# A tuned attention kernel with a new start, row weights in 256 KB pieces, and keys laid out for 512-byte transfers

## The chip, the cores and the metric

The kernel runs on one core of one Trainium2 chip. The profile shows five engines of this core, which run side by side (in the kernel before PE is busy for 77% of the span, ACT for 65%, DVE for 59% and POOL for 53%): PE (matrix multiply), DVE (vector), ACT (activation functions), POOL (general vector work) and SP (here it only starts DMA transfers). The metric is device time of one execution in microseconds (us); lower is better. Executions of one kernel scatter here by about 2% (the kernel before: 413.71 to 422.22 us). A run is called slow when it is more than 1.5% above the fastest of the same kernel, and fast otherwise.

All ratios below are computed in one way: the mean time of one kernel's fast runs over the mean time of the other kernel's fast runs of the same rounds on the same chip. This is not quite the ratio of the medians quoted beside them, which are taken over all runs. The bracket behind a ratio is its 95% interval.

## The reference

Two blocks are run twice in a row on x of 2048 tokens by 512 columns. Block A is attention with 32 heads of 16 columns and a window of 256 keys. Block B changes a single row: it picks the row with the largest score, sends it through a gated MLP (512 to 1792 and back) and adds the result.

```python
def _A_ref(x, wqkv, wo):
    B, S, D = x.shape
    H = 32; Dh = D // H; W = 256
    qkv = (x @ wqkv).reshape(B, S, 3, H, Dh)  # then transposed: 3, B, H, S, Dh
    q, k, v = qkv[0], qkv[1], qkv[2]
    scores = jnp.einsum("bhqd,bhkd->bhqk", q, k) * (Dh ** -0.5)
    mask = (idx[:, None] - idx[None, :] >= 0) & (idx[:, None] - idx[None, :] < W)
    p = _softmax(jnp.where(mask, scores, -1e9))
    return einsum("bhqk,bhkd->bhqd", p, v) ... @ wo
# ...
x = A_x
x = x + _A_ref(_layernorm(x), A_wqkv, A_wo)
x = x + _B_ref(_layernorm(x), B_w_r, B_w_gate, B_w_up, B_w_down)
x = x + _A_ref(_layernorm(x), A_wqkv, A_wo)
x = x + _B_ref(_layernorm(x), B_w_r, B_w_gate, B_w_up, B_w_down)
```

(The transposes of the reference are written here as comments or "...".)

## The kernel before

The kernel does not write its instructions in program order. It registers operations with their data dependencies, an assumed duration (`dur`) and a priority (`prio`, in units of token tiles of 128). A list scheduler in the kernel file then fixes, before anything runs, the order of each engine's queue. That is the order in which each engine is handed its work.

Keys pass through four steps. A projection leaves 256 tokens of keys for eight heads in PSUM, the memory that PE's results go to, as fp32. DVE casts them to bf16 into `KTN`, in SBUF, the memory that holds the operands. DMA transfers scatter each head into `KBD`, which is block-diagonal: 4 heads by 32 keys form the 128 columns of one stationary operand (the side of a matmul that PE loads first, as its weights), and the rows of other heads stay zero. PE loads such a block as weights and multiplies it with the queries.

```python
self.KTN = self.sb("KTN", [128, 2, 2, 4, 256], BF16)
self.KBD = self.sb("KBD", [128, self.RK, 4, 8, 128], BF16)      # 4 groups, 8 key blocks, 4 heads x 32 keys
# ... qk(): the two casts out of PSUM, 28 times each
S.add("dve", lambda e: e.tensor_copy(out=self.QT[:, s, tok], in_=q()), ..., dur=612, name="evq", prio=at - URG)
S.add("dve", lambda e: e.tensor_copy(out=self.KTN[:, kb, :, s, :], in_=k()), ..., dur=612, name="evk", prio=at - URG)
# ... kscat(): eight DMAs of 32 KB, one for each head
dst = self.KBD[rows, k2, :, :, 32 * (h % 4):32 * (h % 4) + 32].rearrange("p s b k -> p (s b) k")   # runs of 32 keys = 64 bytes
src = self.KTN[rows, (pr // 2) % 2, pr % 2].rearrange("p s (b k) -> p (s b) k", k=32)
# ... scores(): 256 query columns; edges(): the same weights with 32 columns
r = e.matmul(self.PS[:, G.bank + x, W * u:W * u + n], lhsT=self.KBD[rows, k2, s, 4 * (T % 2) + b, :],
             rhs=self.QT[rows, s, q0:q0 + n], ...)
```

The MLP weights come in loads of 896 KB. The priorities that are constants: `LEAD = 1.0` (how early scores are placed), `URG = 1.0` (how early DVE empties PSUM), `PVL = 0.5` (how early P times V is placed).

Of the kernel before, what the change touches and what calls it, by code (L numbers as in the profile page):

```python
# [56 lines left out]
class _Op:  # L57
    __slots__ = ("idx", "eng", "fn", "deps", "dur", "name", "is_dma", "prio", "signals", "count",
                 "dma_sem", "start", "end", "waits", "dma_extra", "force", "group")

    def __init__(self, idx, eng, fn, deps, dur, name, is_dma, prio):
        self.idx = idx
        self.eng = eng
        self.fn = fn
        self.deps = deps
        self.dur = dur
        self.name = name
        self.is_dma = is_dma
        self.prio = prio
        self.signals = False  # L70
        self.count = 0
        self.dma_sem = None
        self.start = 0.0
        self.end = 0.0
        self.waits = None
        self.dma_extra = 0.0
        self.force = None
        self.group = None

# [13 lines left out]
class Sched:  # L93
# [8 lines left out]
    def __init__(self, dma_latency=2700.0, sem_latency=100.0, n_dma_slots=48):  # L102
# [17 lines left out]
    def add(self, eng, fn, reads=(), writes=(), banks=(), dur=100.0, name="", is_dma=False, prio=None, extra_deps=(), group=None):  # L120
# [26 lines left out]
        op.group = group  # L147
        if group is not None:
            group.ops.append(idx)
# [24 lines left out]
    def schedule(self):  # L174
# [54 lines left out]
        done = 0  # L229
        while done < n:  # L230
# [29 lines left out]
            busy_end = st + op.dur  # L260
            op.end = busy_end + ((self.dma_latency + op.dma_extra) if op.is_dma else 0.0)
# [106 lines left out]
    def run_engine(self, e, handle, sems, dma_sems):  # L368
# [13 lines left out]
        if e == "sp":  # L382
            totals = {}
            for i in self.dma_ops:
                o = ops[i]
                if totals.get(o.dma_sem, 0) < o.count:
                    totals[o.dma_sem] = o.count
            for slot, tot in sorted(totals.items()):
                if self.sp_known.get(("dma", slot), 0) < tot:
                    handle.wait_ge(dma_sems[slot], tot)  # L390


NBATCH = 4
CAPS = {"s": 2, "m": 3, "q": 4}
LEAD = 1.0
URG = 1.0
MIL = 0.0
PVL = 0.5
# [5 lines left out]
W = 256  # L404
# [3 lines left out]
class Builder:  # L408
# [16 lines left out]
    def alloc(self):  # L425
# [5 lines left out]
        self.RM = 2  # L431
# [3 lines left out]
        self.MW = self.sb("MW", [128, self.RM, FF * 2], BF16)  # L435
# [4 lines left out]
        self.KBD = self.sb("KBD", [128, self.RK, 4, 8, 128], BF16)  # L440
        self.VN = self.sb("VN", [128, 2, 4, 8, 17], BF16)
        self.VBD = self.sb("VBD", [128, self.RV, 8, 2, 8, 17], BF16)
# [45 lines left out]
        self.mctr = 0  # L488
        self.chunks = {}
# [13 lines left out]
    def init(self):  # L503
# [3 lines left out]
        S.base = -9.0  # L507
        self.load_x(0, -9.5)
        for i, c in enumerate((0, 512, 1024)):
            for h in range(2):  # L510
                S.dma("act" if h else "sp", lambda e, c=c, h=h: e.dma_start(self.WQKV[:, 2 * h:2 * h + 2, c:c + 512],
                                                                            self.A_wqkv[256 * h:256 * h + 256, c:c + 512].rearrange("(kc p) n -> p kc n", p=128)),
                      writes=["wqkv%d_%d" % (i, h)], nbytes=256 * 1024, name="ld_wqkv", prio=-9.3 + 0.3 * i)
            if i == 0:
                self.load_x(2, -9.2)

        wo = self.A_wo.rearrange("(sp q x p) n -> sp q p x n", sp=2, q=4, x=2)
        for i in range(8):
            q, sp = i // 2, i % 2
            S.dma("act", lambda e, q=q, sp=sp: e.dma_start(self.WO[32 * q:32 * q + 32, 2 * sp:2 * sp + 2, :], wo[sp, q]), writes=["wo%d" % i],  # L520
                  nbytes=64 * 1024, name="ld_wo", prio=-7.0)
        S.dma("act", lambda e: e.dma_start(self.WR16[:], self.B_w_r.partition_broadcast(128)),
              writes=["wr16"], nbytes=128 * 1024, name="ld_wr", prio=-6.9)
        for g in range(4, self.RX, 2):
            self.load_x(g, -6.8 + 0.1 * g)
        S.add(P, lambda e: e.memset(self.JUNK[:, 0:128], 1.0), writes=["junk"], dur=100)
        S.add(P, lambda e: e.memset(self.ONEB[:], 1.0), writes=["oneb"], dur=60)
        S.add(P, lambda e: e.memset(self.MHALF[:], -0.5), writes=["mhalf"], dur=60)
        S.add(P, lambda e: e.affine_select(out=self.IDB[:], in_=self.JUNK[:, 0:128], pattern=[[-1, 128]], compare_op=ALU.is_equal,
                                           fill=0.0, base=0, channel_multiplier=1), reads=["junk"], writes=["idb"], dur=300)  # L530
        S.base = -8.0
        S.add(P, lambda e: e.affine_select(out=self.M8[:], in_=self.JUNK[:, 0:8].rearrange("p (a h) -> p a h", a=2), pattern=[[-64, 2], [-16, 4]],
                                           compare_op=ALU.is_ge, fill=0.0, base=0, channel_multiplier=1), reads=["junk"], writes=["m8"], dur=100)
        S.add(P, lambda e: e.affine_select(out=self.M8[:], in_=self.M8[:], pattern=[[64, 2], [16, 4]],
                                           compare_op=ALU.is_ge, fill=0.0, base=15, channel_multiplier=-1), reads=[], writes=["m8"], dur=100)
        S.add(P, lambda e: e.tensor_tensor(out=self.M4[:], in0=self.M8[:, 0, :], in1=self.M8[:, 1, :], op=ALU.add), reads=["m8"], writes=["m4"], dur=100)
        S.add(P, lambda e: e.affine_select(out=self.IDF[:], in_=self.JUNK[:, 0:128], pattern=[[-1, 128]], compare_op=ALU.is_equal,
                                           fill=0.0, base=0, channel_multiplier=1), reads=["junk"], writes=["idf"], dur=300, prio=0.4)

        T = self.XN[:, 1, 0:256].rearrange("p (w h k) -> p w h k", w=2, h=4)  # L540
        S.add(P, lambda e: e.memset(self.XN[:, 1, 0:256], 1.0), writes=["xn#1"], dur=120)
        for w, pat, base, cm, op in ((slice(0, 2), [[0, 2], [-32, 4], [0, 32]], 0, 1, ALU.is_ge), (slice(0, 2), [[0, 2], [32, 4], [0, 32]], 31, -1, ALU.is_ge),
                                     (0, [[32, 4], [1, 32]], 0, -1, ALU.is_ge), (1, [[-32, 4], [-1, 32]], 0, 1, ALU.is_gt)):
            v = T[:, w]
            S.add(P, lambda e, v=v, pat=pat, base=base, cm=cm, op=op: e.affine_select(out=v, in_=v, pattern=pat, compare_op=op, fill=0.0, base=base, channel_multiplier=cm),
                  reads=[], writes=["xn#1"], dur=250)
        S.add("dve", lambda e: e.tensor_reduce(out=self.MSK[:], in_=T.rearrange("p w h k -> p w k h"), axis=AX.X, op=ALU.max), reads=["xn#1"], writes=["msk"], dur=350)

        for p in range(1, self.RK):
            S.add("act", lambda e, p=p: e.memzero(self.KBD[:, p].rearrange("p a b c -> p (a b c)")),  # L550
                  writes=["kbd%d_%d" % (p, h) for h in range(32)], dur=2200, name="zkbd", prio=-8.0 + p)
        for p in range(self.RV):
            S.add("dve" if p else P, lambda e, p=p: e.memset(self.VBD[:, p].rearrange("p a b c d -> p (a b c d)"), 0.0),
                  writes=["vbd%d_%d" % (p, h) for h in range(4)], dur=1200, name="zvbd", prio=-3.5 + p)
        S.add(P, lambda e: e.memset(self.VN[:].rearrange("p a b c d -> p (a b c d)"), 1.0),
              writes=["vn0", "vn1"], dur=560, name="ovn", prio=-3.8)
        for q in range(4):
            v = self.PT[:, PITCH * 24 * q:PITCH * 24 * (q + 1)].rearrange("p (n c) -> p n c", c=PITCH)[:, :, 0:96]
            S.add(P, lambda e, v=v: e.memset(v, 0.0), writes=["pz%d" % q], dur=1500, name="zpt", prio=-3.0 + 0.1 * q)
        S.add(P, lambda e: e.memset(self.PT[:, PITCH * 96:PITCH * 96 + 96], 0.0), writes=["pz4"], dur=60, prio=-2.0)  # L560
# [5 lines left out]
              reads=["wr16"], writes=["swc"], dur=600, prio=-0.5)  # L566
# [15 lines left out]
    def ln(self, g, at):  # L582
# [6 lines left out]
        S.add("dve", lambda e: e.bn_stats(out=self.ST6[:, k4, :], in_=x), reads=[xk], writes=["st6#%d" % k4], dur=612, name="bnst")  # L589
        S.add("dve", lambda e: e.bn_aggr(out=MV[:, k4, :], in_=self.ST6[:, k4, :]), reads=["st6#%d" % k4], writes=["mv#%d" % k4], dur=160)  # L590
        rk = "rs#%d" % k4
        S.add("pool", lambda e: e.tensor_scalar(out=RS[:, k4, 0:1], in0=MV[:, k4, 1:2], scalar1=1.0, scalar2=EPS, op0=ALU.mult, op1=ALU.add),
              reads=["mv#%d" % k4], writes=[rk], dur=220)
        S.add("pool", lambda e: e.tensor_tensor(out=RS[:, k4, 1:2], in0=RS[:, k4, 0:1], in1=self.MHALF[:], op=ALU.pow),
              reads=["mhalf"], writes=[rk], dur=560)
# [51 lines left out]
    def qk(self, b, s, at):  # L647
        S = self.S
        kb = b % 2
        XNT = self.XNT  # L650
        G = S.group("m" if b else "q")

        def f(e, ph, js):
            r = None
# [494 lines left out]
    def build(self):  # L1149
# [20 lines left out]
        for b in range(NW // NBATCH):  # L1170
# [9 lines left out]
            if b:  # L1180
                ev(w - 2.08, self.kscat, 2 * b)
# [1041 lines left out]
```

## Time and profile before

| | before |
|---|---|
| time, median of 3 runs | 416.69 us (413.71 to 422.22) |
| profiled span, granted PE clock | 413.4 us, 0.901 |
| first exponential of the softmax | 30.5 us |
| first and last P times V matmul | 35.5 and 388.5 us |
| DMA packets | 137,854 |
| PE idle put down to "issue" | 28.0 us |

The page of the profile gives each engine's busy time. Below that it cuts the span into 40 equal slices, here of 10.3 us: a digit is the busy share in tenths, for PEclk the granted PE clock in tenths of full speed. From the page of the kernel before:

```profile
span 413.4 us, 20980 instructions
PE 316.3 (77%) x9521; PEld 224.8 (54%) x9521; DVE 243.4 (59%) x601; ACT 268.0 (65%) x298; POOL 219.9 (53%) x403
...
PE   0488998769789678897668987888988876877771
...
ACT  2329978877877377885119749748798875869100
...
PEclk9999999999789898999559998869999996959858
DMA  8444425426676954728895193764447485684060
```

PE is busy 77% of the time, and no engine fills the span. At the left edge PE is idle for the whole first slice (the first matmul starts at 14.7 us), and ACT, which does the exponentials, is at two to three tenths for three. The clock has a dip (5) in the middle.

The chain of waits goes back from the last instruction to whatever released each step. The same page sums it by engine, then by line:

```profile
PE 50%; ACT 16%; DVE 12%; issue 8%; DMA 8%; POOL 2%; SPq 1%; DVEq 0%; POOLq 0%
ACT PT L747 16%; PE PS L833 13%; PE PS L659 11%; PE PS L769 9%; PE PS L872 8%; DMA OT<-ON 6%; PE PS L701 6%; DMA XR<-in_A_x_dram 2%; PE PS L798 2%; PE PS L1050 2%; DVE PT L780 1%; DVE JUNK L895 1%; DVE XR L877 1%; DVE ST6M L893 1%; DVE ON L851 1%
```

The groups of instructions with shapes kept apart show what it and its neighbours cost. Columns are line, engine, operation, tiles, shape and count, then busy us and mean ns, then the engine's idle time just before them and what ended it:

```profile
L769 PEld LDWEIGHTS PS<-QT,KBD 64*128 64x128 bf16 x1024 | 39.4, 97 | 54.1 <-ACT PT L747 34.3 <-issue 6.1 <-DVE ON L851 3.4
L798 PE MATMUL PS<-QT,KBD 64*128 64x32 bf16 x896 | 16.4, 175 | 4.6 <-ACT PT L747 2.4 <-issue 2.0
L798 PEld LDWEIGHTS PS<-QT,KBD 64*128 64x128 bf16 x896 | 14.4, 94 | 9.3 <-ACT PT L747 5.9 <-issue 2.2 <-DVE VN L710 0.4
L685 DVE CAST KTN<-PS 128x512 bf16<-128x512 f32 x28 | 19.0, 677 | 0.0
```

So a load of a key block as weights takes 94 to 97 ns, and an edge matmul 175 ns. For the scatter of the keys, the view of one tile gives the time of the issue on SP (min, median and max, ns) and the time from issue to landing:

```profile
L722 SPq DMA_DIRECT2D KBD<-KTN x120: 591/632/3262, 31.8 to 358.7; - x120
DMA to landing us min/median/max: 2.3/3.1/8.0
```

The table by stretches of time has busy us and counts for PE, weight loads, DVE, ACT and POOL, then granted clock, DMA share and GB/s. It shows the dip in the middle:

```profile
200.00:220.00 20.00, 13.43 (x367) 10.86 (x366) 7.78 (x23) 4.95 (x6) 8.23 (x16) 0.53 0.80 174
```

### The profile page before, as it was taken

The numbers are of one execution on the slowest core, as the hardware profiler recorded it, in microseconds if no ns is written. First come the engines' busy times: TensorE is split into PE (matmuls) and PEld (weight loads), VectorE is DVE, ScalarE is ACT, GpSimd is POOL, SyncE is SP. The second block draws the span as 40 slices with busy tenths as digits, with TensorE's granted clock in tenths as the row PEclk, the third lists the DMA queues.
The fourth block names the chain that finished last, engine by engine and source line by source line (L and its number), as shares of the span: only waits on it lengthen the run. The fifth ranks groups of instructions, "written<-read, shape, count | busy, mean of one in ns | idle before, by whom it ended". The sixth has DMA issues, their size and how long they took to land.

```text
span 413.4 us, 20980 instructions
## 1 busy us (share of the span) xinstructions
PE 316.3 (77%) x9521; PEld 224.8 (54%) x9521; DVE 243.4 (59%) x601; ACT 268.0 (65%) x298; POOL 219.9 (53%) x403
## 2 busy tenths in 40 slices
PE   0488998769789678897668987888988876877771
PEld 0244676556567356566455655636665655646540
DVE  6684565566658264795437687627756563527661
ACT  2329978877877377885119749748798875869100
POOL 9992445464863448555144419927595533527231
PEclk9999999999789898999559998869999996959858
DMA  8444425426676954728895193764447485684060
GB/s 243 125 95 88 74 37 132 87 45 110 136 86 163 223 97 118 153 55 242 94 241 111 60 185 69 154 142 137 65 95 154 121 192 70 144 226 117 22 199 23
DMA packets 137854, 50.94 MB, mean 123 GB/s; under 512 B 114073, under 2 KB 132122, under 8 KB 137757
## 3 DMA queue, kind: packets, MB, share of 16 engines
q1 hardware_dynamic: 136156, 48.07, 54.1%
q8 instruction: 77, 1.26, 1.3%
q10 hardware_dynamic: 1600, 1.44, 1.2%
q14 instruction: 21, 0.16, 0.1%
HBM read 24.00 MB, written 13.95 MB: 92 GB/s over the span
## 4 chain that ended last, share of the span: by engine, by line
PE 50%; ACT 16%; DVE 12%; issue 8%; DMA 8%; POOL 2%; SPq 1%; DVEq 0%; POOLq 0%
ACT PT L747 16%; PE PS L833 13%; PE PS L659 11%; PE PS L769 9%; PE PS L872 8%; DMA OT<-ON 6%; PE PS L701 6%; DMA XR<-in_A_x_dram 2%; PE PS L798 2%; PE PS L1050 2%; DVE PT L780 1%; DVE JUNK L895 1%; DVE XR L877 1%; DVE ST6M L893 1%; DVE ON L851 1%
## 5 line engine op out<-in xcount | busy, mean ns | idle before, releaser
L747 ACT ACTIVATE PT<-PS 128x1024 bf16<-128x1024 f32 (+5 forms) x284 | 258.7, 999 | 96.0 <-PE PS L769 93.1
L833 PE MATMUL PS<-VBD,PT 64*128 64x34 bf16 x5760 | 103.2, 177 | 22.5 <-issue 14.9
L769 PE MATMUL PS<-QT,KBD 64*128 64x256 bf16 (+4 forms) x1024 | 100.6, 279 | 24.6 <-ACT PT L747 15.1
L833 PEld LDWEIGHTS PS<-VBD,PT 64*128 64x128 bf16 x5760 | 97.7, 94 | 39.2 <-issue 21.0
L807 POOL TENSOR_TENSOR PT<-PT,MSK 128x1024 bf16<-128x1024 bf16 x28 | 59.2, 2114 | 41.3 <-ACT PT L747 41.0
L659 PE MATMUL PS<-XNT,WQKV 64*128 64x512 bf16 x512 | 75.4, 387 | 2.2 <-DVE MV L590 1.7
L769 PEld LDWEIGHTS PS<-QT,KBD 64*128 64x128 bf16 x1024 | 39.4, 97 | 54.1 <-ACT PT L747 34.3
L899 POOL TENSOR_SCALAR RSM<-XR 128x1 f32<-128x1 f32 x32 | 9.9, 308 | 103.0 <-DVE XR L894 99.2
L780 DVE TENSOR_TENSOR PT<-PT,MSK 128x512 bf16<-128x512 bf16 x64 | 30.8, 481 | 45.5 <-ACT PT L747 45.3
L872 PE MATMUL PS<-WO,OT 64*128 64x256 bf16 x512 | 46.7, 304 | 12.2 <-DMA OT<-ON 8.7
L701 PE MATMUL PS<-WQKV,XNT 64*128 64x256 bf16 x512 | 47.4, 297 | 4.1 <-issue 3.3
L877 DVE TENSOR_TENSOR XR<-PS,XR 128x512 f32<-128x512 f32 x32 | 22.0, 689 | 29.5 <-PE PS L872 29.5
L872 PEld LDWEIGHTS PS<-WO,OT 64*128 64x128 bf16 x512 | 25.6, 104 | 22.2 <-DMA OT<-ON 9.6
L849 DVE RECIPROCAL RD<-PS 128x16 f32<-128x16 f32 x64 | 15.9, 249 | 34.0 <-PE PS L833 31.8
L659 PEld LDWEIGHTS PS<-XNT,WQKV 64*128 64x128 bf16 x512 | 25.1, 96 | 16.3 <-issue 4.8
L710 DVE CAST VN<-PS 128x512 bf16<-128x512 f32 x32 | 22.0, 689 | 18.4 <-PE PS L701 18.4
L701 PEld LDWEIGHTS PS<-WQKV,XNT 64*128 64x128 bf16 x512 | 25.0, 102 | 13.7 <-issue 4.6
L683 DVE CAST QT<-PS 128x512 bf16<-128x512 f32 x28 | 19.2, 686 | 16.3 <-PE PS L659 16.3
L851 DVE TENSOR_TENSOR ON<-PS,RD 128x256 bf16<-128x256 f32 x64 | 26.9, 420 | 1.2
L895 DVE SCALAR_TENSOR_TENSOR JUNK<-XR,WR 128x512 bf16<-128x512 f32 x32 | 24.6, 768 | 0.0
L602 POOL TENSOR_SCALAR XN<-XR,RS 128x512 bf16<-128x512 f32 (+1 forms) x28 | 22.6, 811 | 2.1 <-DMA XNT<-XN 1.3
L589 DVE BATCH_NORM_STATS2 ST<-XR 128x6 f32<-128x512 bf16 (+1 forms) x32 | 20.9, 672 | 2.9 <-DMA XR<-in_A_x_dram 2.9
(106 smaller groups left out, 289.9 us busy)
## 6 DMA issues: line engine op xcount, KB each, us to landing
scr<-XR SPq DMA_DIRECT2D x13, 516.0 KB, 4.1
vd<-VN SPq DMA_DIRECT2D x16, 272.0 KB, 3.6
VBD<-vd SPq DMA_DIRECT2D x64, 68.0 KB, 2.9
XR<-scr SPq DMA_DIRECT2D x8, 512.0 KB, 4.4
KBD<-KTN SPq DMA_DIRECT2D x120, 32.0 KB, 3.1
MW<-in_B_w_gate_dram SPq DMA_DIRECT2D x4, 896.0 KB, 5.3
MW<-in_B_w_down_dram SPq DMA_DIRECT2D x4, 896.0 KB, 7.3
XR<-in_A_x_dram SPq DMA_DIRECT2D x8, 256.0 KB, 6.7
```

The source lines that it names most:

```text
L602: S.add("pool", lambda e: e.tensor_scalar(out=XN[:, k2, :], in0=x, scalar1=RS[:, k4, 1:2], scalar2=RS[:, k4, 2:3], op0=ALU.mult, op1=ALU.add),
L659: r = e.matmul(self.PS[:, G.bank + w, :], lhsT=self.WQKV[rows, j, 512 * w + 128 * s:512 * w + 128 * s + 128], rhs=XNT[rows, kb, :, j, :], ...
L701: r = e.matmul(o, lhsT=XNT[rows, kb, jt, j, :], rhs=self.WQKV[rows, j, 1024 + 256 * w:1280 + 256 * w], start=(ph == 0 and j == 0), stop=(p ...
L747: return e.activation(out=out, in_=i, func=ACTF.Exp, scale=0.25)
L769: r = e.matmul(self.PS[:, G.bank + x, W * u:W * u + n], lhsT=self.KBD[rows, k2, s, 4 * (T % 2) + b, :], rhs=self.QT[rows, s, q0:q0 + n], s ...
L780: S.add("dve", lambda e: e.tensor_tensor(out=P, in0=P, in1=m, op=ALU.mult), reads=["msk"], writes=["pt%d_%d" % ((4 * t + b) % 12, 2 * sp + ...
L807: S.add("pool", lambda e: e.tensor_tensor(out=P[:, :, :, 0:32], in0=P[:, :, :, 0:32], in1=m, op=ALU.mult), reads=["msk"], writes=key, dur= ...
L833: r = e.matmul(self.PS[:, G.bank + x, 34 * g:34 * g + 34], lhsT=self.PT[rows, c:c + 128], rhs=self.VBD[rows, v3, b8, :, 2 * s + a, :], sta ...
L851: S.add("dve", lambda e: e.tensor_tensor(out=o, in0=acc()[:, :, :, 0:16], in1=rd.unsqueeze(3).broadcast_to([128, 2, 8, 16]), op=ALU.mult), ...
L872: r = e.matmul(self.PS[:, G.bank + w, 0:256], lhsT=self.OT[rows, k2, j, :], rhs=self.WO[rows, j, 256 * w:256 * w + 256], start=(ph == 0 an ...
L877: S.add("dve", lambda e: e.tensor_tensor(out=self.xf(T).rearrange("p (x c) -> p x c", x=2), in0=self.PS[:, G.bank:G.bank + 2, 0:256], in1= ...
L895: S.add("dve", lambda e: e.scalar_tensor_tensor(out=self.JUNK[:], in0=x, scalar=1.0, in1=self.WR16[:], op0=ALU.mult, op1=ALU.mult, accum_o ...
```

## The change

The intent is to start earlier, to shorten DMA work and to keep the queues fed:

1. Start: the first batch's queries and keys are projected in two halves, each after two row tiles; 16 matmuls on constants keep PE busy during the loads; zeroing is done as 32-bit words; small layer-norm operations go from POOL to DVE.
2. Row (MLP) weights come as 256 KB pieces into 7 buffers and, near the end, into space that has come free.
3. Keys are interleaved, key by key, over the eight blocks of 32, so that the scatter moves 512 bytes at a time in place of 64.
4. Order: new priorities, and the scheduler gets a model of instruction fetch, with constants of its own (13.6 ns an instruction).

The diff is cut to its core; parts that only rename or set assumed durations are left out.

```diff
-        self.KBD = self.sb("KBD", [128, self.RK, 4, 8, 128], BF16)
+        self.KBD = self.sb("KBD", [128, self.RK, 4, 4, 256], BF16)
 # ... qk(): the cast of the keys
-        S.add("dve", lambda e: e.tensor_copy(out=self.KTN[:, kb, :, s, :], in_=k()), ..., dur=612, name="evk", prio=at - URG)
+        S.add("dve", lambda e: e.tensor_copy(out=self.KTN[:, kb, :, s, :].rearrange("p a (k b) -> p a b k", b=8), in_=k()), ..., dur=600, name="evk", prio=at - URG)
 # ... the block as PE loads it
+    def keys(self, rows, k2, s, b):
+        return self.KBD[rows, k2, s].rearrange("p h (k b) -> p (h k) b", b=8)[:, :, b]
 # ... kscat()
-                dst = self.KBD[rows, k2, :, :, 32 * (h % 4):32 * (h % 4) + 32].rearrange("p s b k -> p (s b) k")
-                src = self.KTN[rows, (pr // 2) % 2, pr % 2].rearrange("p s (b k) -> p (s b) k", k=32)
+                dst = self.KBD[rows, k2, :, h % 4, :]
+                src = self.KTN[rows, (pr // 2) % 2, pr % 2]
 # ... the first batch in halves, and PE kept busy
+            def warm(e, G=G):
+                for _ in range(4):
+                    r = e.matmul(self.PS[:, G.bank, :], lhsT=self.JUNK[:, 0:128], rhs=self.JUNK[:], start=True, stop=True)
+    def qk_first(self, half, s, at):
 # ... row weights
-        self.MW = self.sb("MW", [128, self.RM, FF * 2], BF16)
+        self.MW = self.sb("MW", [128, 7, 1024], BF16)
 # ... order of the queues
+FETCH_NS = 13.6
+FETCH_AHEAD = 512
-LEAD = 1.0
-URG = 1.0
-MIL = 0.0
-PVL = 0.5
+LEAD = 2.188
+URG = 1.942
+MIL = -0.471
+PVL = 0.507
```

## The prediction

> **What bounds the kernel now** (median 416.7 us, profiled span 413.4). No single engine: the page's busy table has PE 316 us (77%), ACT 268, DVE 243, POOL 220, and the chain of waits is 50% PE, 16% ACT, 12% DVE, 8% "issue", 8% DMA. Time is lost in four places.
>
> 1. Start. The timeline has no matmul before 14.7 us and the first softmax exponential at 30.5. POOL is 9.4 of the first 10 us busy: 2.02 us memsets stand in front of the tiny layer-norm operations, and Q/K of the first batch waits for all four row tiles (PE begins it at 22.3).
> 2. Row-weight loads. They come as two 896 KB DMAs; an attention-output transpose queued behind them took 8.4 us (at 132) and 8.8 us (at 334), against a median of 4.0. PE sat 4.4 us, then ran on.
> 3. Between 194 and 214 the timeline has PE gaps of 2.1, 3.5 and 3.6 us put down to "issue". The stretch table shows PE 13.4 of 20 us busy at a granted clock of 0.53 in 200–220, with the DMA engines saturated just before (1.23 of an engine share, an overlap artefact). [...] The waits view sums PE issue gaps to 28 us.
> 4. Clock. 0.66–0.69 in 110–120, 270–280, 340–350, 0.60 in 360–370: about 20 us of PE busy time runs longer than it need. [...]
>
> **What the change does**
> - Start: 32-bit memsets (1.87–2.02 → about 1.0 us), eps additions on DVE instead of POOL (308 ns POOL → about 0.15), Q/K after two tiles, weights before other loads, 16 warming matmuls. My estimate, from load landings of 5–9 us and 0.85 us per half group: exponentials flow from about 17 us. Gain 13 us, carried through, since what follows is a full pipeline.
> - Key scatter: 64 B runs become 512 B; 120 DMAs × 512 = 61,000 of the 138,000 packets become 7,700. DMA share falls from 54% of 16 engines to about 40%; issue shrinks from 0.63 to about 0.45 us each.
> - Row weights in 256 KB: transposes wait about 1 us, not 4–5. With fewer packets and instruction-aware PE ordering I expect half of items 2–4 back: 13 us.
> - Tail: most down-weights are already there (before, PE waits 1.9 us for them and ends the second down product at 406.8); the final DMA wait moves behind the flag. 4 us.
> - Added: 64 small DVE operations (about 10 us DVE, off the chain), warm matmuls 4–7 us in idle PE, and key weights read with a 16-byte stride: 1,920 weight loads, in this trace 94–97 ns each. [...] The 256-column scores should hide it, the 32-column edges (16 us) may not: 0–10 us, expected 2.
>
> Sum: −13 −13 −4 +2 = −28, so **388 us**, 80% range 373–403. Faster by over 2%: 0.92; within 2%: 0.06; slower: 0.02.
>
> **Right if**: first exponential by 15–19 us; packets near 84,000; PE issue gaps under 16 us; no 20 us stretch at 0.53; output transposes never over 6 us; edge and score groups within 10% busy.
>
> **Wrong if**: strided weight loads double and show as PE time in the edge groups; the earlier start is eaten by an ACT-limited middle; new piece loads collide elsewhere; clock dips move rather than vanish.

Three passages are cut out of it where marked: what the author took to be the cause of the "issue" gaps and of the halved clock, and why strided weight reads should cost time. What the reads do cost was measured afterwards: 150 to 162 ns a load in place of 94 to 97. That half of items 2 to 4 would come back (the second 13), and the +2, were estimates, with no measurement behind them. The "about 20 us" of item 4 is an estimate too: in its four stretches of 10 us, busy time times the clock that is missing comes to about 10 us, and with 200 to 220 to 16. The figures for the change are forecasts; the kernel after has 0.97 us (DVE) and 1.07 us (POOL) for a memset, 0.14 us for an addition on DVE and 0.60 us for an issue of the scatter (medians).

## The result, and the profile after

| | before | after |
|---|---|---|
| time, median | 418.65 us (413.71 to 422.22, 4 runs) | 459.95 us (459.38 to 465.47, 4 runs) |
| ratio | | 1.1108 [1.0948, 1.1268] |
| profiled span, granted clock | 413.4 us, 0.901 | 457.6 us, 0.851 |
| first exponential | 30.5 us | 20.2 us |
| first and last P times V matmul | 35.5 and 388.5 us | 48.5 and 436.6 us |
| DMA packets | 137,854 | 94,813 |
| PE idle put down to "issue" | 28.0 us | 14.4 us |

The median of before differs from the one given above because one more run was taken beside the new kernel. The changed kernel is 11% slower. All four of its runs are fast; of the four of before, the two above 420 us count as slow, so the ratio rests on 413.71 and 416.69 us. The lines that answer to those of before begin with its page; a slice is now 11.4 us:

```profile
span 457.6 us, 21192 instructions
PE 359.3 (79%) x9601; PEld 267.9 (59%) x9601; DVE 296.7 (65%) x676; ACT 273.0 (60%) x303; POOL 194.2 (42%) x334
...
PE   4967977887888779987897866986789786985782
...
ACT  4488236778887487754176524785386768794300
...
PEclk9787789899999997789559987689978999795677
DMA  8423423324257335814596336364545421559041
```

The left edge has filled up as intended. DVE, though, went from 243.4 to 296.7 us. The chain of waits of the kernel after, by engine and by line:

```profile
PE 53%; DVE 28%; ACT 11%; issue 5%; DMA 2%; SPq 0%; DVEq 0%
DVE KTN L717 14%; PE PS L834 11%; PE PS L898 11%; ACT PT L812 11%; PE PS L703 8%; PE PS L762 7%; PE PS L937 6%; PE PS L863 5%; DVE QT L715 4%; PE PS L1178 2%; DVE XR L942 2%; DMA XR<-in_A_x_dram 2%; PE PS L1132 1%; DVE PT L845 1%; DVE KTN L743 1%
```

DVE's share of the chain went from 12% to 28%, and a line that did not show before, the key cast (now line 717), is its largest single term: 14% of 457.6 is 64 us. Taken in order of time, the chain runs through all 28 of these casts. The groups of the kernel after, for the same instructions as before (scores are line 834 now, edges 863, P times V 898, exponentials 812):

```profile
L834 PEld LDWEIGHTS PS<-QT,KBD 64*128 64x128 bf16 x1024 | 61.9, 150 | 72.0 <-ACT PT L812 25.9 <-DVE KTN L717 14.0 <-issue 6.6
L863 PE MATMUL PS<-QT,KBD 64*128 64x32 bf16 x896 | 32.6, 212 | 5.9 <-issue 3.3 <-ACT PT L812 2.5
L863 PEld LDWEIGHTS PS<-QT,KBD 64*128 64x128 bf16 x896 | 31.2, 162 | 9.8 <-ACT PT L812 5.3 <-issue 3.7
L717 DVE CAST KTN<-PS 128x512 bf16<-128x512 f32 x28 | 68.3, 2439 | 0.0
```

One cast takes 2439 in place of 677 ns, so 28 of them are busy 68.3 in place of 19.0 us. Weight loads of keys went from 94–97 to 150–162 ns, and an edge matmul from 175 to 212 ns. The last columns of the score loads already name the cast: 14.0 us of idle time in front of them end with it. A stretch of the chain in order of time (start, us, what) from the kernel after shows how the cast delays PE:

```profile
69.39 0.60 DVE JUNK L962 x2
69.99 0.10 DVE XR L959
70.09 0.57 DVE QT L715
70.66 2.33 DVE KTN L717
...
73.05 0.44 PE PS L834 x4
```

The casts of queries and keys run one behind the other on DVE and PE's scores start when the key cast ends. The view of line 717 sums who waited for it (us, times):

```profile
  PEld PS L834: 14.0, 9
  PE PS L834: 12.2, 9
  PEld PS L898: 4.4, 3
  PE PS L898: 3.8, 3
```

ACT suffers behind PE: its waits for scores went from 93.1 to 127.7 us in the waits view. The key scatter, in the view of its tile, did become cheaper:

```profile
L787 SPq DMA_DIRECT2D KBD<-KTN x120: 590/597/1929, 28.4 to 405.0; - x120
DMA to landing us min/median/max: 2.0/2.6/4.5
```

The dip of the clock is still there, in a later stretch:

```profile
220.00:240.00 20.00, 18.27 (x432) 13.74 (x426) 8.38 (x31) 9.44 (x13) 9.28 (x16) 0.51 0.92 231
```

### The profile page after: what moved, and what is told of

Its sections match the earlier page's. It is cut to its first block, busy times and chain, and to the rows that moved or that the text cites. A ratio compares the mean times of both kernels' runs of the same rounds, so it can differ in the third digit from the quotient of the medians.

```text
span 457.6 us, 21192 instructions
## 1 busy us (share of the span) xinstructions
PE 359.3 (79%) x9601; PEld 267.9 (59%) x9601; DVE 296.7 (65%) x676; ACT 273.0 (60%) x303; POOL 194.2 (42%) x334
## 2 busy tenths in 40 slices
DMA packets 94813, 50.93 MB, mean 111 GB/s; under 512 B 53112, under 2 KB 89081, under 8 KB 94716
## 4 chain that ended last, share of the span: by engine, by line
PE 53%; DVE 28%; ACT 11%; issue 5%; DMA 2%; SPq 0%; DVEq 0%
DVE KTN L717 14%; PE PS L834 11%; PE PS L898 11%; ACT PT L812 11%; PE PS L703 8%; PE PS L762 7%; PE PS L937 6%; PE PS L863 5%; DVE QT L715 4%; PE PS L1178 2%; DVE XR L942 2%; DMA XR<-in_A_x_dram 2%; PE PS L1132 1%; DVE PT L845 1%; DVE KTN L743 1%
## 5 line engine op out<-in xcount | busy, mean ns | idle before, releaser
L812 ACT ACTIVATE PT<-PS 128x1024 bf16<-128x1024 f32 (+5 forms) x284 | 263.3, 986 | 145.2 <-PE PS L834 127.7
L834 PE MATMUL PS<-QT,KBD 64*128 64x256 bf16 (+4 forms) x1024 | 114.7, 311 | 42.6 <-ACT PT L812 13.4
L834 PEld LDWEIGHTS PS<-QT,KBD 64*128 64x128 bf16 x1024 | 61.9, 150 | 72.0 <-ACT PT L812 25.9
L961 POOL TENSOR_TENSOR XR<-XR,MHALF 128x1 f32<-128x1 f32 x32 | 17.8, 555 | 135.0 <-DVE XR L960 123.1
L703 PE MATMUL PS<-XNT,WQKV 64*128 64x512 bf16 x448 | 67.7, 388 | 5.5 <-DVE KTN L717 2.9
L717 DVE CAST KTN<-PS 128x512 bf16<-128x512 f32 x28 | 68.3, 2439 | 0.0
L937 PE MATMUL PS<-WO,OT 64*128 64x256 bf16 x512 | 48.5, 305 | 5.5 <-DVE KTN L717 2.9
L762 PEld LDWEIGHTS PS<-WQKV,XNT 64*128 64x128 bf16 x512 | 28.8, 111 | 15.7 <-issue 5.4
L863 PE MATMUL PS<-QT,KBD 64*128 64x32 bf16 x896 | 32.6, 212 | 5.9 <-issue 3.3
L863 PEld LDWEIGHTS PS<-QT,KBD 64*128 64x128 bf16 x896 | 31.2, 162 | 9.8 <-ACT PT L812 5.3
L771 DVE CAST VN<-PS 128x512 bf16<-128x512 f32 x32 | 22.2, 700 | 16.6 <-PE PS L762 16.4
L703 PEld LDWEIGHTS PS<-XNT,WQKV 64*128 64x128 bf16 x448 | 21.6, 97 | 18.6 <-DVE KTN L717 3.5
L638 POOL TENSOR_TENSOR RS<-RS,MHALF 128x1 f32<-128x1 f32 x32 | 18.6, 592 | 28.5 <-DVE MV L634 18.5
```

The costliest lines, as they stand in the source:

```text
L703: r = e.matmul(self.PS[:, G.bank + w, :], lhsT=self.WQKV[rows, j, 512 * w + 128 * s:512 * w + 128 * s + 128], rhs=XNT[rows, kb, :, j, :], ...
L762: r = e.matmul(o, lhsT=XNT[rows, kb, jt, j, :], rhs=self.WQKV[rows, j, 1024 + 256 * w:1280 + 256 * w], start=(ph == 0 and j == 0), stop=(p ...
L812: return e.activation(out=out, in_=i, func=ACTF.Exp, scale=0.25)
L863: r = e.matmul(self.PS[:, G.bank + x, c:c + 32], lhsT=self.keys(rows, k2, s, 4 * (T % 2) + bb), rhs=self.QT[rows, s, q0:q0 + 32], start=(b ...
L937: r = e.matmul(self.PS[:, G.bank + w, 0:256], lhsT=self.OT[rows, k2, j, :], rhs=self.WO[rows, j, 256 * w:256 * w + 256], start=(ph == 0 an ...
```

## The experiments

The first theory is that the cast's writes with a 16-byte step cost the time. The rival theories are that the weights read with a 16-byte step cost it, or that the new start or the new order does. Eighteen kernels ran, in five sets; the kernel before was run with each set (medians 418.83, 417.02, 418.56 and 418.16 us in the timed ones), and every kernel gave the reference's result. Line 717 is the key cast in all kernels made from the one after, line 685 in those made from the one before.

### Only the cast's direction changed

```diff
-  tensor_copy(out=self.KTN[:, kb, :, s, :].rearrange("p a (k b) -> p a b k", b=8), in_=k())
+  tensor_copy(out=self.KTN[:, kb, :, s, :].rearrange("p a (k b) -> p a k b", b=8), in_=k().rearrange("p a b k -> p a k b"))
```

The first batch's cast was changed in the same way. Layout, weights, transfers and the order of every queue are those of the kernel after; only now the writes are contiguous and the reads from PSUM take the step.

> The changed kernel, but the cast of the keys walks its elements in the other order: it reads PSUM with a stride and writes SBUF contiguously. Layout, DMA runs of 512 B and weight stride of 16 B stay, the result stays right. Theory A (the strided SBUF write of the key cast, 2439 ns instead of 677, 28 times, is the loss): cast back at 0.7 us, time 380 to 405 us, ratio to before 0.91 to 0.97. Rival B (the strided weight loads slow the PE): cast at 0.7 us but time still over 435. Rival C (new order and pieces are what lose): over 445.

Measured: 410.64 us (407.57 to 415.31), 0.9778 [0.9677, 0.9878] of before. The groups of this kernel:

```profile
L863 PEld LDWEIGHTS PS<-QT,KBD 64*128 64x128 bf16 x896 | 30.8, 163 | 9.9 <-ACT PT L812 5.8 <-issue 3.4
L717 DVE CAST KTN<-PS 128x512 bf16<-128x512 f32 x28 | 19.1, 681 | 0.0
```

The cast is back at 681 ns although the step is now on the PSUM side, and 49.3 us of the median are gone (459.95 less 410.64). The weight loads still cost 163 ns. So the cast carries the loss, and the strided weights do not. The time is a little over the 380 to 405 us that theory A expected, and far under the 435 and 445 of its rivals.

### The new layout alone, on the kernel before, with and without the strided cast

```diff
 # kernel before, with the KBD, keys() and kscat() of the change
+  tensor_copy(out=self.KTN[:, kb, :, s, :].rearrange("p a (k b) -> p a b k", b=8), in_=k())                              # first
+  tensor_copy(out=self.KTN[:, kb, :, s, :].rearrange("p a (k b) -> p a k b", b=8), in_=k().rearrange("p a b k -> p a k b"))  # second
```

> The kernel before with the changed key layout alone (512 B runs, strided cast, strided weights). A and B: 450 to 475 us, ratio 1.08 to 1.14, since 28 casts get 1.76 us longer (49 us on DVE) in a kernel whose other queues are as before. C: within 2% of before.

> As e4, but with the cast writing contiguously. A: 400 to 418 us, ratio 0.96 to 1.0, as the 512 B runs help a little. B: 445 or more, close to e4.

Measured: 469.17 us, 1.1144 [1.1007, 1.1281], with the strided cast, and 421.82 us, 1.0108 [1.0021, 1.0194], with contiguous writes. From the groups of the first of the two:

```profile
L685 DVE CAST KTN<-PS 128x512 bf16<-128x512 f32 x28 | 68.2, 2436 | 0.0
```

Nearly all of the 11% comes with the cast, even with old start, old order and old row loads; 47.4 us of it goes when the writes are contiguous. The second kernel also prices the rest of the layout: packets fall by 53,761 to 84,093 and the main queue's share from 54.1% to 50.0%, and yet the time rises by about 1%, while PE's loads of key weights take 149 to 163 ns each. The layout is no gain at all on the kernel before, where theory A had expected a small one, 400 to 418 us: the cast was right, this part was not.

### All of the change but the layout

```diff
 # kernel after, with KTN, KBD, kscat() and the weights of the kernel before
-        return self.KBD[rows, k2, s].rearrange("p h (k b) -> p (h k) b", b=8)[:, :, b]
+        return self.KBD[rows, k2, s, b, :]
```

> The changed kernel with the old key layout whole: 64 B runs, contiguous casts and weights; all else stays changed. A and B: 380 to 405 us. C: over 430. Against e1 it tells what 512 B runs gain less what strided weights cost: A expects the two within 2%; B expects this one 30 us or more below e1. Weight loads of the scores back to 97 ns from 150, of the edges to 94 from 162.

Measured: 405.42 us (403.66 to 408.67), 0.9727 [0.9637, 0.9816]. The queues are in the order of the kernel after. This is 5.2 us below the kernel with contiguous casts, though the intervals overlap. The rest of the change is thus worth about 2.7% (1.8 to 3.6% by the interval), or 11 us of the predicted 28 or so. This kernel is called "old keys" below, and the question becomes where the rest went.

### Middle ways: four and two blocks interleaved

```diff
 # kernel after, contiguous casts; D = 4, then D = 2
-        self.KBD = self.sb("KBD", [128, self.RK, 4, 4, 256], BF16)
+        self.KBD = self.sb("KBD", [128, self.RK, 4, 8 // D, 4, 32 * D], BF16)
-        return self.KBD[rows, k2, s].rearrange("p h (k b) -> p (h k) b", b=8)[:, :, b]
+        return self.KBD[rows, k2, s, b // D].rearrange("p h (k d) -> p (h k) d", d=D)[:, :, b % D]
```

> The changed kernel with keys interleaved four blocks at a time instead of eight: 256 B runs, weights read with a stride of 8 B, casts written contiguously; result right. If the 16-byte stride (one key per 16 bytes) is what slows the weight loads, score loads fall from 149 ns to about 98 and edge loads from 163 to about 94, PE busy from 350 to about 325, time 395 to 405 us. If any stride does it, they stay near 149 and 163 and the time at 405 to 412.

> As the run with four blocks interleaved, with two: 128 B runs, weights read with a stride of 4 B. If only strides that leave fewer than four keys to 16 bytes are slow: score loads 97 to 100 ns (four blocks 116, eight 149), edges 94 to 97, and 400 to 406 us, the fastest so far or level with it.

Measured: 406.05 us, 0.9705 [0.9618, 0.9792], with four blocks (runs of 256 bytes, weights at a step of 8 bytes), and 411.28 us, 0.9879 [0.9764, 0.9993], with two (128 bytes, 4 bytes). The second has 12 first-batch DVE operations more than old keys. Four blocks is level with old keys, and it is the only kernel of those run in rounds whose whole interval lies below 0.98. Two expectations missed: with four blocks the loads went neither back to 98 and 94 ns nor stayed at 149 and 163 (116 and 114), and two blocks, whose loads did come back (98 and 95), took 411.28 us and not the 400 to 406. From the groups of the four-block kernel:

```profile
L840 PEld LDWEIGHTS PS<-QT,KBD 64*128 64x128 bf16 x1024 | 47.9, 116 | 54.0 <-ACT PT L818 30.9 <-issue 7.2 <-DVE QT L715 2.4
```

The mean weight load of the scores was 98 ns with a step of 2 bytes (old keys), 98 with 4, 116 with 8 and 149 with 16.

### Where the write gets dear

```diff
 # four-block and two-block kernels, the key cast iterated so that it writes with a step of 2 * D bytes
-  out=self.KTN[...].rearrange("p a (c k d) -> p a c k d", k=32, d=D), in_=k().rearrange("p a (c d) k -> p a c k d", d=D)
+  out=self.KTN[...].rearrange("p a (c k d) -> p a c d k", k=32, d=D), in_=k().rearrange("p a (c d) k -> p a c d k", d=D)
```

> The four-block kernel (406.05 us, cast 680 ns with contiguous writes) with its key cast iterated so that each step writes 8 bytes further in SBUF (PSUM read in order). If the write cost goes with how far apart two writes lie (16 bytes cost 2439 ns): about half the excess, 1500 to 1700 ns a cast. If any write that isn't contiguous costs the same: about 2440 ns, and about 455 us. If only 16 bytes and more cost: about 680 ns, and 402 to 412 us.

> The same for two interleaved blocks (411.3 us, cast 680 ns with contiguous writes): each step of the cast writes 4 bytes further. If the cost goes with the distance: 900 to 1200 ns. If any write that isn't contiguous costs the same: about 2440 ns, and about 455 us. If only 16 bytes and more cost: about 680 ns, and 405 to 416 us.

Measured: 414.99 us with a step of 8 bytes and 402.96 us with 4 bytes, single runs. Their groups, in this order, one from each kernel:

```profile
L717 DVE CAST KTN<-PS 128x512 bf16<-128x512 f32 x28 | 36.3, 1298 | 0.0
```

```profile
L717 DVE CAST KTN<-PS 128x512 bf16<-128x512 f32 x28 | 20.2, 722 | 0.0
```

A cast of 512 columns takes 680 ns with contiguous writes, 722 with a step of 4 bytes, 1298 with 8 and 2439 with 16. At 8 bytes all three expectations missed: the excess is neither half of that at 16 bytes nor all of it nor none, but a third (618 of 1759 ns). At 4 bytes the third came nearest. From 4 to 8 bytes the cast takes 1.80 times as long, from 8 to 16 bytes 1.88 times; up to 4 bytes only 1.06 times. These are four points: why the cost rises so is not shown, and what a step beyond 16 bytes costs is open, since no run has one.

### Each remaining part undone in the kernel with old keys

```diff
 # old order
-FETCH_NS = 13.6                      +FETCH_NS = 0.0
-LEAD = 2.188, URG = 1.942, MIL = -0.471, PVL = 0.507      +LEAD = 1.0, URG = 1.0, MIL = 0.0, PVL = 0.5   (and the other priorities and assumed DMA latency of before)
 # old row loads: load_mlp, mlp_gu, mlp_act and mlp_down of before, 896 KB each
 # old start: init() of before, the first batch projected whole, V early
```

> The run with the old key layout (405 us) with the old priorities and without the model of instruction fetch in the order of the queues; start and pieces stay changed. If the new order is worth the gain in the middle that the prediction put on it: 410 to 420 us. If the order gives nothing: 402 to 408, and PE idle put down to issue stays within 5 us of that run's.

> The run with the old key layout with the old 896 KB row weight loads; all else as there. If the pieces are worth what the prediction expected [...]: 412 to 420 us and output transposes over 8 us again. If they give little: 402 to 408.

> The run with the old key layout with the old start (loads, memsets, whole first batch, no warming matmuls); all else as there. If the earlier start goes through to the end: first exponential at 29 to 31 us and 413 to 420 us. If the head start is lost soon after (in that run ACT idles 7.1 and 4.2 us between 44 and 59 us while PE does projections): 403 to 409.

Measured: 415.32 us, 0.999 [0.9917, 1.0064], with the old order; 417.59 us, 1.0036 [0.9957, 1.0115], with the old row loads; 417.36 us, 0.9947 [0.9852, 1.0043], with the old start (two of its four runs were slow, the profiled one among them, so its ratio rests on two runs and its trace is not used). The old order leaves PE's "issue" idle time where it was (19.9 us, 19.1 in old keys), and with the old row loads the slowest output transpose lands in 8.5 us again, as expected. Whichever part is taken out, the whole 2.7% goes. Parts whose gains add up do not behave so.

### Single parts put into the kernel before

```diff
 # kernel before with init(), the halves of the first batch and the layer norm of the change
 # kernel before with the 256 KB pieces of the change
```

> The kernel before with the new start alone. If the start's 11 us go through: 403 to 408 us (0.97 to 0.98), first exponential at 19 to 21 us. If the head start is lost later without the other parts: 413 to 420.

> The kernel before with the 256 KB row weight pieces alone. If they are worth 3% by themselves: 402 to 408 us, no output transpose over 7 us and no stretch of 20 us at a granted clock near 0.53. If they pay only together with the new order: 412 to 420.

Measured: 420.06 us, 1.0052 [0.9941, 1.0164], with the new start; 420.33 us, 1.0031 [0.9896, 1.0166], with the pieces. Neither gives anything by itself, though the new start does bring the first exponential from 30.5 to 20.4 us.

### Two priorities nudged

```diff
 # old keys                                   # kernel before
-LEAD = 2.188, PVL = 0.507                    -LEAD = 1.0, PVL = 0.5
+LEAD = 2.1,   PVL = 0.49                     +LEAD = 1.04, PVL = 0.483
```

> The run with the old key layout (405 us), with nothing changed but two priorities by a few per cent (the lead of the scores 2.188 to 2.1, that of PV 0.507 to 0.49): same work, same start, same pieces, a slightly other order. If start, pieces and order are worth 2 to 3% each by themselves: 402 to 408 us. If the order is fitted to the exact program, so that any edit costs what the undone parts cost: 412 to 418.

> The kernel before with two priorities of its order nudged by 3 to 4% (LEAD 1.0 to 1.04, PVL 0.5 to 0.483). If the order of the kernel before is as closely fitted as that of the changed kernel with old keys: slower by 2 to 4%, 428 to 435 us. If it is an ordinary order: 412 to 424 us.

Measured: old keys nudged 420.24 us, 1.0082 [0.999, 1.0174]; before nudged 424.44 us, 1.0183 [1.0088, 1.0279]. A nudge of 3 to 4% in two constants, with no work added or removed, costs old keys its whole gain, 3.6% against its own ratio and more than the 412 to 418 us that the worse expectation gave, and before 1.8%. The second lies under the 2% that was expected of a closely fitted order, and above an ordinary one's; it is between the two readings.

### PE kept busy for longer, and for less long

```diff
-                for _ in range(4):      # 16 warming matmuls in four groups
+                for _ in range(9):      # 36;  in the other kernel range(1): 4
```

> The kernel with the old key layout (405.4 us) with 36 warm-up matmuls in place of 16, which fill the idle gap of 4.3 us after them; the order of every queue is unchanged. If the low clock of the start costs time: mean granted clock of 10 to 20 us rises from 0.83 to 1.0 and the kernel is 1 to 3 us faster. If the start's clock is off the critical path: within 2 us of 405.

> The same kernel with 4 warm-up matmuls in place of 16, every queue's order unchanged. If warming matters: slower by 1 to 4 us. If the 16 matmuls do nothing for the time: level with 405 within 1 us.

Measured: 409.73 us, 0.9801 [0.9693, 0.9909], with 36, and 406.42 us, 0.9774 [0.9685, 0.9862], with 4. The stretch from 10 to 20 us, first of old keys, then of the kernel with 36:

```profile
10.00:20.00 10.00, 8.09 (x136) 6.82 (x138) 9.07 (x21) 5.21 (x9) 4.15 (x8) 0.83 0.66 148
```

```profile
10.00:20.00 10.00, 9.12 (x150) 6.76 (x148) 9.04 (x21) 5.35 (x9) 4.14 (x8) 1.00 0.62 142
```

With 36 the granted clock in this stretch is 1.00 in place of 0.83, and the kernel is not faster; its median is above what either expectation gave, by no more than the intervals leave open. In old keys an idle gap of 4.1 us lies behind the 16 matmuls (the expectation has 4.3), and the clock is at half from 11.4 to 14.8 us, after it. It is at half from 28.4 to 35.2 us too, without such a gap: PE's longest between 20 and 28.4 us is 1.4 us. And the column can't be read in the first stretch of every run: with 4 warming matmuls it shows 1.00 from 10 to 20 us, but the first eight projections there take 1.03 us, as in old keys (1.04), against 0.61 with 36; the kernel before, with none, shows 1.00 there as well and takes 1.04 us for eight of them from 17.9 us on. The scores first start at 20.0 us with 4, 18.8 with 16 and 18.7 with 36, which hold the first transposes back from 10.6 to 12.2 us. So neither a slower nor a faster clock in the start shows in the time beyond the noise, and the warming matmuls buy nothing that can be measured.

### V ahead of queries and keys in the start

In old keys, V of the first batch is stored at 27.4 us, against 21.2 us before, and the first P times V comes at 41.7 us. One theory was that late V uses up the head start.

```diff
-  ev(-0.4 + 0.2 * j, self.vproj, j)
+  ev(-3.2 + 0.05 * j if j < 2 else -0.4 + 0.2 * j, self.vproj, j)
-  ev((w - 1.4) if b else -0.15, self.vscat, 2 * b, at=w + AT["vs0"] if b else -0.15)
+  ev((w - 1.4) if b else -2.9, self.vscat, 2 * b, at=w + AT["vs0"] if b else -4.0)
```

> The same kernel (405.4 us) with the V chain of the first two tiles ahead of their Q and K chains. If the late V ate the head start of the exponentials: first PV matmul at 30 to 35 us in place of 41.7, more than 33 exponentials by 60 us in place of 30, and 395 to 404 us. If the gain of 2.7% sits in a fitted order alone, this change of order loses it: 412 to 420 us.

Measured: 411.47 us, 0.9857 [0.9762, 0.9952]. The blocks of V are now loaded from 19.2 us on (32.0 in old keys), and the first P times V still starts at 40.9 us. The timeline of PE in this kernel (start, us, line, operation, tiles, shape, count) shows what it does instead:

```profile
38.67 0.38 PE L834 MATMUL PS<-QT,KBD 64*128 64x256 bf16 x4
38.89 0.81 PE L703 MATMUL PS<-XNT,WQKV 64*128 64x512 bf16 x6
39.53 0.38 PE L834 MATMUL PS<-QT,KBD 64*128 64x256 bf16 x4
39.76 0.82 PE L703 MATMUL PS<-XNT,WQKV 64*128 64x512 bf16 x6
...
40.85 0.56 PE L898 MATMUL PS<-VBD,PT 64*128 64x34 bf16 x32
```

PE is busy with scores and with the projections of the second batch (line 703), which its queue has in front. So late V is not the limit, and that theory falls. The time lies between the two expectations, and nearer to the second: half of the gain is lost.

## Why the prediction was right or wrong

Its time, 388 us, and its range, up to 403, were wrong, and so was the direction. The miss of 72.0 us can be split with medians: 49.3 us from the kernel after to the same with contiguous casts, 5.2 us from there to old keys, and 17.4 us from old keys to 388. The medians of the first step come from different sets of runs, so the split is good to a few us.

**The step that failed: "Added: 64 small DVE operations (about 10 us DVE, off the chain), warm matmuls 4–7 us in idle PE, and key weights read with a 16-byte stride".** The list asks what reads the new layout and not what has to write it. The cast was taken as unchanged. It costs 49 us more on DVE, and two kernels show that it delays the whole by about as much: 49.3 us in the changed kernel and 47.4 in the kernel before by the medians (51.6 and 45.2 by the means of the fast runs). Nearly all of it lies on the critical path although DVE is 65% busy, because the casts stand directly between a projection and the scores; the chain runs through them (14% of it in the kernel after, the largest line). How much a better order could hide is open: the scheduler still took the cast for 600 ns, and no run gave it the 2439. The prediction counted the step of 16 bytes as a possible cost of PE's reads alone. For DVE's writes the runs show it: a cast took 1298 ns at a step of 8 bytes and 2439 at 16, against 680 with contiguous writes.

**"key weights read with a 16-byte stride: ... 0–10 us, expected 2": the size was about right.** Loads went from 94–97 to 150–162 ns and edges from 16.4 to 32.6 us and scores from 100.6 to 114.7 us of PE time, both outside the 10% that was named; the edges doubled, as its "Wrong if" had it. Yet the net cost is about 1% on the kernel before, and 5.2 us, not resolved, on the changed one.

**"Key scatter: 64 B runs become 512 B": right in the counts, empty in time.** It removed 53,761 packets, just the change from 512 to 64 packets in each of 120 DMAs, and landing fell from 3.1 to 2.6 us. The main queue's share fell by 4 points with the same bytes (54.1% to 50.0%, on the kernel before), but about 40% was predicted, and no kernel with longer runs was faster than old keys by more than the noise. The scatter was not what ended the waits: in the kernel before, no wait at all is put down to it. The packets missed "near 84,000" because the 256 KB pieces add 10,719 (148,573 with the pieces alone, on the kernel before), and 84,093 with the 10,719 is 94,812 of the 94,813 counted.

**"Start: ... Gain 13 us, carried through": half right, then the sign was wrong.** The first exponential came at 20.2 us (19.2 in old keys), a little after the 15–19 that was predicted. But what counts is when the pipeline of scores, exponentials and P times V runs, and this began later, not earlier. The profiles, in us:

| kernel | to the first P times V | from there to the last | after it |
|---|---|---|---|
| before | 35.5 | 353.0 | 24.9 |
| before, new start | 40.5 | 354.0 | 25.2 |
| before, pieces | 36.5 | 358.0 | 24.7 |
| after | 48.5 | 388.1 | 21.0 |
| old keys | 41.7 | 339.9 | 20.3 |
| four blocks | 43.8 | 340.3 | 20.5 |
| old keys, old order | 40.3 | 348.7 | 21.9 |
| old keys, old row loads | 41.7 | 348.6 | 24.5 |
| old keys, nudged | 42.2 | 353.9 | 21.4 |
| old keys, V first | 40.9 | 348.1 | 21.4 |

With the new start, PE does more scores early, and between 40 and 60 us old keys has ACT busy 8.7 us of 20, against 18.3 us before (14.8 with the new start alone, 14.7 in old keys with the old order, so the new order has the larger share in it). By 60 us ACT has issued 28 exponentials in old keys and 30 in before. The head start is paid back there and in the first P times V, which comes 5 to 6 us later. The prediction's own warning, "eaten by an ACT-limited middle", points at the right stretch; but ACT is not the limit in it: between 44 and 59 us it is idle for 7.1 and 4.2 us until PE delivers scores.

**"Row weights ... and instruction-aware PE ordering ...: 13 us": the size came out in old keys, the reason was not shown.** The middle is 13.1 us shorter there; that this is the 13 of the prediction is luck. It was put down to shorter waits for DMA and to the order of PE's queue. In the kernel after, PE's "issue" gaps did shrink, from 28.0 to 14.4 us (under the 16 that was named), and the transposes' median landing fell from 4.0 to 2.7 us, with a maximum of 6.3 us in place of 8.8 (over the 6 that was named). In old keys, where the gain is, they are 19.1, 3.7 and 6.7 us. PE's waits for these transposes did fall there, from 8.7 to 1.1 us. But with the old row loads they stay low (1.6 us) and the gain is gone all the same. The middle of 340 us is found only with the exact order: it stays with 36 and with 4 warming matmuls (340.5 and 338.6 us), and the nudge loses it while the transfers and the scheduler's fetch model stay. Undoing the priorities and the fetch model together moves the "issue" gaps only from 19.1 to 19.9 us, so what causes these gaps is not shown either. What makes the one order better than its neighbours is open.

**"Tail: ... 4 us": right.** What follows the last P times V takes 24.9 us before, 21.0 after and 20.3 in old keys. With the old row loads it is 24.5, so the pieces are needed; but pieces alone, on the kernel before, leave it at 24.7. The wait of 1.9 us that the prediction put down to the down-weights is one for DVE in the trace (`BAD`, line 1132); that for the weights is 1.4 us.

**"Wrong if: ... clock dips move rather than vanish": they moved.** The stretch at 0.53 from 200 to 220 us became one at 0.51 from 220 to 240. What causes them is open. In the kernel before, the granted clock halves at 198.1 us, while PE's gap of 3.5 us there runs from 199.1 to 202.6 and only one of 2.1 us lies before it; so the long gap did not bring that dip about.

So the changed kernel's sum, by the table of stretches, is +13.0 before the first P times V, +35.1 in the middle and −3.9 at the end, 44.2 us together. The cast alone accounts for about 49; without the layout the same three are +6.2, −13.1 and −4.6.

## What to carry to other kernels

When a layout is changed to please one reader, list every instruction that writes it as well as those that read it, and give each a measured duration: here the cost sat in a cast that nobody had changed on purpose, and turning its iteration round, so that the step falls on the PSUM read, took it away (2439 to 681 ns a cast, 49.3 us of the median). Count an earlier start only when the slowest stage behind it starts earlier too, so watch the first P times V and not the first exponential. Where the order of static queues is fitted, a change of 2 to 4% from a single part can be nothing but the order (here the nudges cost 3.6 and 1.8%), so nudge a constant that moves no work before crediting a part.
